# Noisy top-2 experts on one core: a round's last sums and product written behind the next round's first copy

## The chip, the cores and the metric

The kernel runs on one core of one Trainium2 chip. Times are device microseconds (us) of one execution; the figure for a kernel is the median of its runs. The engines are TensorE (PE, with its weight loads as PEld), VectorE (DVE), ScalarE (ACT), GpSimd (POOL) and SyncE (SP, which issues DMAs here).

## What is computed

Three layers follow each other on 2304 tokens of width 512: windowed attention, a gated MLP, and a mixture of eight experts of which each token takes two. The change lies in the third layer alone:

```
def _moe2_ref(x, w_gate, w_noise, noise, w1, w2):
    noisy_logits = x @ w_gate + np.log1p(np.exp(x @ w_noise)) * noise
    top2 = np.argpartition(-noisy_logits, 2, axis=1)[:, :2]
    ...                                   # top2_w: softmax over the two
    for e in range(E):                    # 8 experts, w1[e]: 512 x 1024, w2[e]: 1024 x 512
        for k in range(2):
            mask = top2[:, k] == e
            h = np.maximum(x[mask] @ w1[e], 0.0)
            out[mask] += top2_w[mask, k, None] * (h @ w2[e])
```

Matrix operands are held as a pair, a rounded high part and the remainder ("hi" and "lo"), and each product is three matmuls: hi·hi, hi·lo, lo·hi.

## The kernel before, in words

Each expert takes up to 608 rows (five blocks j = 0 to 4 of 128, the last of 96). They are gathered from DRAM by GpSimd (`gather`), turned by TensorE into columns (`gt`: four 128x128 transposes a block, copied out by ScalarE at L916), multiplied by w1 and put through a relu into `h2` (tile hTa), multiplied by w2 (`p2`, 24 matmuls a block with 512 columns, L315 to L317), scaled into the rows read back from the output (L970, or L972 for expert 0) and scattered (L974).

Expert 0 computes its first product directly (`p1(0, f, groups)`, L932). Blocks 0 to 2 are done by then; what stands here is group 1 (blocks 3 and 4): eight tiles f, each 12 matmuls of 224 columns, a ScalarE relu (L938) and a VectorE remainder (L939).

Experts 1 to 7 use a scheme with seven products in place of eight (`Seven`). Rows and weights are halved both ways; `sums` (L1169 to L1172) makes four sums of row quarters, `operands` (L1116 on ScalarE, then L1117 on VectorE) splits them into hi and lo, and `prep` does the same for the weights: a w1 tile has four small sums on VectorE (L1144 to L1147) and four splits, a w2 tile has two splits. `some(n)` writes the next n pieces of prepared weight work into the order. A product P1 to P7 is six matmuls of 304 columns (L1191). `Seven.p1(e, i)` is one **round** of seven products; an expert has four rounds. Their results combine by accumulation in PSUM and by copies on ScalarE:

- P1 into bank A; ScalarE copies A to B_ (L1208), since P6 then goes on adding into A and P2 adds into B_.
- P7 into Z; ScalarE copies it to an SBUF buffer `u` (L1213).
- After P6, A is copied to C (L1216); P4 adds into C. After P5, A is copied to D_ (L1222); P3 adds into D_.
- Four outputs: B_ itself; A plus the copy of Z (L1223 on VectorE); C plus the copy of Z (L1226); D_. Each gets a relu on ScalarE (L1200) and a remainder on VectorE (L1201).

In the kernel before, a round ends with P4, the sum L1226 and its relu; P3 is written at the end of the round (rounds 0 and 3) or behind the next round's P1 (rounds 1 and 2), with `self.rest` holding its relu. `second(e)` is the stretch between two experts: five blocks of `p2`, the transposes of the next expert's rows, its sums and splits, and three weight tiles of the next expert.

From L1239 on, the orders of TensorE, ScalarE and VectorE are exactly the written order (`manual_schedule`); those of GpSimd and SyncE are set by the scheduler. PSUM has eight banks, given out by `bank(i)`; a new tile in a bank waits for the last reader of the one before it.

Of the kernel before, what the change touches and what calls it, by code (L numbers as in the profile page):

```python
# [9 lines left out]
F32 = mybir.dt.float32  # L10
# [5 lines left out]
AF = mybir.ActivationFunctionType  # L16
OP = mybir.AluOpType
# [12 lines left out]
def tile_alibi_window_attention__swiglu__noisy_top2_moe(  # L30
# [1038 lines left out]
    class Seven:  # L1069
# [3 lines left out]
        def __init__(self):  # L1073
            self.xr = wpool[3].tile([128, KC, CW], F32, name="xr")
            n = 2 * HS
            s = wpool[3].tile([128, 4 * n], F32, name="xs")
            self.s = [s[:, i * n:(i + 1) * n].rearrange("p (c t) -> p c t", c=2) for i in range(4)]
            self.g = [s[:, i * RW:(i + 1) * RW] for i in range(4)]
            u = wpool[3].tile([128, 2 * HS], F32, name="us")
            self.u = [u[:, 0:HS], u[:, HS:]]  # L1080
            self.t = hB[:, PB * DM:PB * DM + 1024].rearrange("p (o k f) -> p o k f", o=4, k=2)
            z = NF2 * CW
            self.wb = [([hT[:, i, z:z + 512] for i in range(2)], [hT[:, i, z + 512:z + 768] for i in range(2)])]
            self.wa, self.w2, self.w2t = [], {}, None
            self.jobs = ([("w1", 1, i) for i in range(3)] +
                         [j for e in range(1, E) for j in
                          [("w2", e, 0), ("w2", e, 1), ("w1", e, 3), ("w2", e, 2), ("w2", e, 3)] + [("w1", e + 1, i) for i in range(3) if e + 1 < E]])
            self.nl = self.nj = 0
            self.rest = lambda: None
            self.todo = []  # L1090
            self.raw = {}
# [39 lines left out]
        def prep(self):  # L1131

            if self.nj == len(self.jobs):
                return
            self.load(self.nj + 1)
            what, e, i = self.jobs[self.nj]
            r = self.raw.pop(self.nj)
            self.nj += 1
            if what == "w1":
                a, b, c = w = self.w1_operands((e - 1) * 4 + i)  # L1140
                t = self.t

                def first():
                    nc.vector.tensor_sub(t[:, 0], r[:, 0:2, 1], r[:, 0:2, 0])  # L1144
                    nc.vector.tensor_sub(t[:, 1], r[:, 2:4, 1], t[:, 0])  # L1145
                    nc.vector.tensor_sub(t[:, 2], r[:, 2:4, 1], r[:, 0:2, 1])
                    nc.vector.tensor_sub(t[:, 3], r[:, 2:4, 0], t[:, 1])  # L1147
                    self.split([a[:, s, 0:2].rearrange("p o k f -> p (o k) f") for s in range(2)], r[:, :, 0])
                self.todo += [first, lambda: self.split([a[:, s, 2:4] for s in range(2)], t[:, 0:2]),
                              lambda: self.split(b, t[:, 2:4]), lambda: self.split(c, r[:, 2:4, 1])]  # L1150
                self.w2["w1", e, i] = w
            else:
                t = place1(0) if i < 3 else self.w2t
                self.todo += [lambda u=u: self.split([t[:, u, s, :] for s in range(2)], r[:, u]) for u in range(2)]
                for u in range(2):
                    self.w2[e, 2 * i + u] = t[:, u]
            f = self.todo.pop()
            self.todo.append(lambda: (f(), self.load(self.nj + 2)))
# [35 lines left out]
        def p1(self, e, i):  # L1194
            A, Z, B_, C, D_ = (bank(x)[:, 0:HS] for x in ((6, 7, 0, 1, 4), (2, 3, 5, 6, 7), (0, 1, 2, 3, 4), (5, 6, 7, 0, 1))[i])
            lo, hi = slice(0, HS), slice(HS, CW)

            def out(ps, f, sl):
                d = h2[0][:, f, sl]
                nc.scalar.activation(d, ps, AF.Relu)  # L1200
                nc.vector.scalar_tensor_tensor(h2[1][:, f, sl], ps, 0.0, f32(d), op0=OP.max, op1=OP.subtract)  # L1201

            def last():
                self.product(e, i, "P3", D_, False)
                self.rest = lambda: out(D_, 4 + i, lo)

            self.product(e, i, "P1", A, True)
            nc.scalar.activation(B_, A, AF.Copy)  # L1208
            if i in (2, 3):
                self.last()  # L1210
            self.rest()
            self.product(e, i, "P7", Z, True)
            nc.scalar.activation(self.u[1], Z, AF.Copy)  # L1213
            self.some(1)
            self.product(e, i, "P6", A, False)
            nc.scalar.activation(C, A, AF.Copy)  # L1216
            self.some(1)
            self.product(e, i, "P2", B_, False)
            out(B_, i, lo)
            self.some(1)  # L1220
            self.product(e, i, "P5", A, False)
            nc.scalar.activation(D_, A, AF.Copy)  # L1222
            nc.vector.tensor_tensor(self.u[0], A, self.u[1], op=OP.add)  # L1223
            out(self.u[0], 4 + i, hi)
            self.product(e, i, "P4", C, False)
            nc.vector.tensor_tensor(self.u[1], C, self.u[1], op=OP.add)  # L1226
            out(self.u[1], i, hi)
            if i in (0, 3):
                last()
                if i == 3:  # L1230
                    self.rest()
                    self.rest = lambda: None
            else:
                self.last = last

    sv = Seven()
    for j in range(CAP):
# [2 lines left out]
    by_hand.__enter__()  # L1240
    for f in range(NF2):
        p1(0, f, (1,))
        if f == 3:
            sv.prep()
        sv.some(1)
    sv.some(9)
    sv.open()

    def second(e):
        n = e + 1  # L1250
        more = n < E
        if more:
            gt(n, 0, bank(6))
            gt(n, 1, bank(7))
        j0 = 0 if e else EARLY
        p2(e, j0, 0, 4)
        if more:
            gt(n, 2, bank(6))
            gt(n, 3, bank(7))
        p2(e, j0, 4, 8)  # L1260
        if more:
            sv.operands(0)
            gt(n, 4, bank(6))
            sv.sums()
            for i in (3, 2):
                sv.operands(i)
        p2(e, j0 + 1)
        if more:
            for i in (1, 5, 4):
                sv.operands(i)  # L1270
            sv.prep()
            sv.some(9)
        for j in range(j0 + 2, CAP):
            p2(e, j)
            if more and j < 4:
                sv.prep()
                sv.some(9)
        if more and e == 0:
            sv.prep()
            sv.some(9)  # L1280

    for j in range(EARLY, CAP):
        prev(0, j)
    second(0)
    for e in range(1, E):
        for i in range(4):
            for _ in range(2 if i == 0 else 1):
                sv.prep()
            sv.p1(e, i)
            if i == 1:  # L1290
                for j in range(CAP):
                    prev(e, j)
                if e + 1 < E:
                    for j in range(CAP):
                        gather(e + 1, j)
        sv.some(9)
        second(e)
    by_hand.__exit__(None, None, None)
    w3p_cm.__exit__(None, None, None)
# [73 lines left out]
```

## Time and profile before

| | |
|---|---|
| median of 3 runs | 1108.96 us (1108.17 to 1109.45) |
| the profiled execution | 1107.09 us, of which the span of instructions is 1105.1 us |
| mean granted TensorE clock | 0.986 |
| PE busy | 1055.2 us, 95% |
| DVE busy | 690.6 us, 62% |
| ACT busy | 560.3 us, 51% |
| POOL busy | 345.1 us, 31% |

The busy shares are of the span. Idle times in the rows further down are those of one engine just before an instruction, with what ended them behind an arrow. A matmul's end in the trace is modelled and reaches into the next matmul's start, so that the distance between two starts, not the sum of busy times, tells the pace. The expert layer fills the span from about 620 us on; the part that the change touches begins with group 1 of expert 0 at 670.65 us.

### The profile page before, as it was taken

To read this page: it belongs to the slowest core of one execution; us is meant where nothing else is said; L and a number is where in the kernel's file an instruction comes from. 1 tells how busy PE (TensorE), PEld (TensorE's weight loads), DVE (VectorE), ACT (ScalarE), POOL (GpSimd) and SP (SyncE) were. 2 spreads that over 40 slices of the span, in tenths; PEclk is the share of its full clock that TensorE was granted. 3 is DMA by queue.
4 is the path that set the end of the run, shared out by engine and by line. 5 is a ranking of instruction groups with operands and counts; after the bars stand their busy time and mean duration, and the time that the engine had idled before them with its cause. 6 is when DMAs were issued, how large, how long until landed. Compare 5 with 4: busy or idle time off the path is not lost. (4 is left out here: it accounts for less than half of the span.)

```text
span 1105.1 us, 18329 instructions
## 1 busy us (share of the span) xinstructions
PE 1055.2 (95%) x6830; PEld 900.2 (81%) x6830; DVE 690.6 (62%) x1546; ACT 560.3 (51%) x1283; POOL 345.1 (31%) x324
## 2 busy tenths in 40 slices
PE   6889999999999999999999999699999999999997
PEld 5667778889988777789997888688888888888885
DVE  6778963577620577325885353868686868686861
ACT  6877854455522455444532323555555555556450
POOL 7300002122233333332377123615151515151211
PEclk9899999999999999999999999899999999999999
DMA  9688745232373233241323503525353535353321
GB/s 213 177 242 271 248 156 185 71 90 72 90 240 124 88 96 100 76 129 58 97 93 104 167 12 102 171 87 177 101 179 107 174 107 176 112 166 120 113 75 41
DMA packets 140259, 143.92 MB, mean 130 GB/s; under 512 B 66510, under 2 KB 109518, under 8 KB 140160
## 3 DMA queue, kind: packets, MB, share of 16 engines
q1 hardware_dynamic: 129776, 113.09, 34.4%
q0 software_dynamic: 9184, 29.26, 8.1%
q8 instruction: 56, 0.92, 0.4%
q10 hardware_dynamic: 1200, 0.30, 0.1%
q14 instruction: 43, 0.35, 0.1%
HBM read 113.84 MB, written 28.91 MB: 129 GB/s over the span
## 5 line engine op out<-in xcount | busy, mean ns | idle before, releaser
L296 POOL TENSOR_TENSOR wu<-wst,wu 128x1024 fp32r<-128x1024 f32 x54 | 129.8, 2404 | 265.7 <-ACT wu L295 240.2
L315 PE MATMUL b<-xT,wu 128*128 128x320 f32 (+1 forms) x576 | 200.0, 351 | 4.6 <-ACT xT L525 4.5
L316 PE MATMUL b<-xT,wu 128*128 128x320 f32 (+1 forms) x576 | 197.5, 343 | 0.1
L317 PE MATMUL b<-xT,wu 128*128 128x320 f32 (+1 forms) x576 | 196.6, 342 | 0.0
L315 PE MATMUL b<-wu,hTa 128*128 128x512 f32 (+1 forms) x482 | 192.1, 401 | 0.0
L316 PE MATMUL b<-wu,hTa 128*128 128x512 f32 (+1 forms) x482 | 189.7, 394 | 0.0
L317 PE MATMUL b<-wu,hTa 128*128 128x512 f32 (+1 forms) x482 | 189.5, 394 | 0.0
L1191 PE MATMUL b<-xT,wu 128*128 128x304 f32 x834 | 128.9, 308 | 21.8 <-ACT b L1208 21.8
L1191 PEld LDWEIGHTS b<-xT,wu 128*128 128x128 f32 x834 | 120.3, 191 | 27.9 <-ACT b L1208 27.0
L295 ACT ACTIVATE wu<-wst 128x1024 fp32r<-128x1024 f32 x80 | 84.4, 1057 | 85.2 <-PE b L317 69.2
L315 PEld LDWEIGHTS b<-xT,wu 128*128 128x128 f32 x576 | 107.8, 188 | 16.8 <-ACT xT L525 5.9
L316 PEld LDWEIGHTS b<-xT,wu 128*128 128x128 f32 x576 | 109.1, 189 | 9.7 <-issue 1.6
L317 PEld LDWEIGHTS b<-xT,wu 128*128 128x128 f32 x576 | 109.0, 189 | 9.0 <-issue 1.5
L317 PEld LDWEIGHTS b<-wu,hTa 128*128 128x128 f32 (+1 forms) x482 | 88.8, 184 | 22.2 <-issue 0.3
L315 PEld LDWEIGHTS b<-wu,hTa 128*128 128x128 f32 (+1 forms) x482 | 88.9, 185 | 21.1 <-issue 0.9
L316 PEld LDWEIGHTS b<-wu,hTa 128*128 128x128 f32 (+1 forms) x482 | 89.1, 185 | 20.8 <-issue 0.6
L610 DVE TENSOR_TENSOR hTa<-sg,hTa 128x320 fp32r<-128x320 f32 (+1 forms) x54 | 69.0, 1283 | 23.0 <-ACT hTa L609 22.9
L974 POOL DMA_INDIRECT out_dram<-hTb,sib x39 | 44.4, 1139 | 98.6 <-DVE hTb L970 64.0
L1117 DVE TENSOR_TENSOR wu<-wst,wu 128x512 fp32r<-128x512 f32 x93 | 61.6, 662 | 21.7 <-ACT wu L1116 21.4
L424 ACT ACTIVATE sx<-sx,mn 128x192 f32<-128x192 f32 (+2 forms) x126 | 53.6, 427 | 41.3 <-DVE mn L421 40.9
L970 DVE SCALAR_TENSOR_TENSOR hTb<-b,wcol,hTb 128x512 f32<-128x512 f32 (+1 forms) x35 | 26.1, 747 | 57.6 <-PE b L317 57.6
L1116 ACT ACTIVATE wu<-wst 128x512 fp32r<-128x512 f32 x93 | 55.4, 600 | 0.0
(244 smaller groups left out, 1834.6 us busy)
## 6 DMA issues: line engine op xcount, KB each, us to landing
wst<-wscr SPq DMA_DIRECT2D x54, 512.0 KB, 3.4
wst<-in_moe_w_dram SPq DMA_DIRECT2D x36, 512.0 KB, 3.8
wst<-in_moe_w_dram SPq DMA_DIRECT2D x56, 256.0 KB, 3.2
wscr<-wst SPq DMA_DIRECT2D x18, 512.0 KB, 3.2
cs<-in_moe_w_gate_dram SPq DMA_DIRECT2D x12, 512.0 KB, 5.0
cs<-in_moe_w_val_dram SPq DMA_DIRECT2D x12, 512.0 KB, 6.3
cs<-in_moe_w_out_dram SPq DMA_DIRECT2D x12, 512.0 KB, 5.3
x2d<-xT SPq DMA_DIRECT2D x18, 256.0 KB, 3.2
```

What stands on the lines that cost most here:

```text
L295: nc.scalar.activation(o[0], s, AF.Copy)
L296: self.eng(n).tensor_sub(o[1], s, f32(o[0]))
L315: nc.tensor.matmul(ps, st(0), mv(0), start=first, stop=False, skip_group_check=True)
L316: nc.tensor.matmul(ps, st(0), mv(1), start=False, stop=False, skip_group_check=True)
L317: nc.tensor.matmul(ps, st(1), mv(0), start=False, stop=last, skip_group_check=True)
L424: a = nc.scalar.activation(x, x, AF.Exp, scale=-1.0, bias=mn[:, i:i + 1], accum_out=sm[:, i:i + 1])
L610: nc.vector.tensor_sub(hh(1, f, sl), t, f32(hh(0, f, sl)))
L970: nc.vector.scalar_tensor_tensor(x, y, wc, x, op0=OP.mult, op1=OP.add)
L974: s = nc.gpsimd.indirect_dma_start(out=out, out_offset=bass.IndirectOffsetOnAxis(ap=R["s"][0:r, col:col + 1], axis=0), in_=x, in_offset=No ...
L1116: nc.scalar.activation(o[0], src, AF.Copy)
L1117: nc.vector.tensor_sub(o[1], src, f32(o[0]))
L1191: nc.tensor.matmul(ps, w[k][:, c], x[:, m, c], start=first and c == 0 and k + m == 0, stop=c == 1 and k == 1, skip_group_check=True)
```

## The change

A round no longer ends with the sum into the second `u`, its relu and (in rounds 0 and 3) P3. These go into `rest`, which the next round runs behind its P1 and the copy L1208; after round 3, `second(e)` runs it behind the first two transposed blocks of the next expert. The copy of Z gets two buffers in turn, so that it lives into the next round. Weight work is spread differently: four preparations in place of five lie in an expert's rounds, and that of w2 tile 3 moves to the start of `second`; the third `some` of a round stands between the sum of A and its relu and is left out in round 1; the first piece of a w1 tile is now the four sums alone with the split of the raw quarter as a piece of its own. At the start, expert 1's rows are transposed between the tiles of expert 0's group 1, and its `sums` and splits follow at once; expert 0's last two blocks of `p2` then run beside the splits of expert 1's rows and weights.

```
@@ Seven.__init__
-            u = wpool[3].tile([128, 2 * HS], F32, name="us")
-            self.u = [u[:, 0:HS], u[:, HS:]]
+            u = wpool[3].tile([128, 3 * HS], F32, name="us")
+            self.u = [u[:, i * HS:(i + 1) * HS] for i in range(3)]
@@ prep
-                    self.split([a[:, s, 0:2].rearrange("p o k f -> p (o k) f") for s in range(2)], r[:, :, 0])
-                self.todo += [first, lambda: self.split([a[:, s, 2:4] for s in range(2)], t[:, 0:2]),
+                self.todo += [first, lambda: self.split([a[:, s, 0:2].rearrange("p o k f -> p (o k) f") for s in range(2)], r[:, :, 0]),
+                              lambda: self.split([a[:, s, 2:4] for s in range(2)], t[:, 0:2]),
                               lambda: self.split(b, t[:, 2:4]), lambda: self.split(c, r[:, 2:4, 1])]
@@ Seven.p1
+            u, z = self.u[0], self.u[1 + i % 2]
-            def last():
+            def rest():
+                nc.vector.tensor_tensor(z, C, z, op=OP.add)
+                out(z, i, hi)
                 self.product(e, i, "P3", D_, False)
-                self.rest = lambda: out(D_, 4 + i, lo)
+                out(D_, 4 + i, lo)
+                self.rest = lambda: None
             self.product(e, i, "P1", A, True)
             nc.scalar.activation(B_, A, AF.Copy)
-            if i in (2, 3):
-                self.last()
             self.rest()
             self.product(e, i, "P7", Z, True)
-            nc.scalar.activation(self.u[1], Z, AF.Copy)
+            nc.scalar.activation(z, Z, AF.Copy)
...
             out(B_, i, lo)
-            self.some(1)
             self.product(e, i, "P5", A, False)
             nc.scalar.activation(D_, A, AF.Copy)
-            nc.vector.tensor_tensor(self.u[0], A, self.u[1], op=OP.add)
-            out(self.u[0], 4 + i, hi)
+            nc.vector.tensor_tensor(u, A, z, op=OP.add)
+            self.some(i != 1)
+            out(u, 4 + i, hi)
             self.product(e, i, "P4", C, False)
-            nc.vector.tensor_tensor(self.u[1], C, self.u[1], op=OP.add)
-            out(self.u[1], i, hi)
-            if i in (0, 3):
-                last()
...
+            self.rest = rest
@@ expert 0's group 1
     for f in range(NF2):
         p1(0, f, (1,))
+        if f in (3, 5):
+            gt(1, f - 3, bank(6))
+            gt(1, f - 2, bank(7))
         if f == 3:
             sv.prep()
-        sv.some(1)
+        if f > 3:
+            sv.some(1)
+        if f == 6:
+            gt(1, 4, bank(6))
+            sv.sums()
     sv.some(9)
     sv.open()
+    sv.operands(0)
+    sv.operands(3)
+    sv.operands(2)
+    prev(0, 3)
+    p2(0, 3)
+    for i in (1, 5, 4):
+        sv.operands(i)
+    sv.prep()
+    sv.some(9)
+    prev(0, 4)
+    p2(0, 4, 0, 4)
+    sv.prep()
+    sv.some(9)
+    p2(0, 4, 4, 8)
@@ second(e), now for e of 1 and above only
+        sv.rest()
+        sv.prep()
+        sv.some(9)
+        p2(e, 0, 0, 4)
...
-            for _ in range(2 if i == 0 else 1):
+            for _ in range((2, 1, 0, 1)[i]):
                 sv.prep()
             sv.p1(e, i)
```

One line is added above `p1`, so that its later lines stand a few numbers further down in the changed kernel: L1208 becomes L1212, L1213 L1215, L1216 L1218, L1222 L1223, L1223 L1224, L1226 L1205, L1200 L1201 and L1201 L1202.

**TensorE from expert 0's group 1 on**, before (a name such as b_6897 is a PSUM bank's tile; the rows of L932 are the tiles f of group 1, those of L913 the transposed blocks of expert 1; xT holds split rows, wu split weights, hTa the remainders and `h2`):

```order
L932 MATMUL b_6897<-xT_6205,wu_6141 128x224 x12
L932 MATMUL b_6914<-xT_6205,wu_6141 128x224 x12
L932 MATMUL b_6931<-xT_6205,wu_6303 128x224 x12
L932 MATMUL b_6954<-xT_6205,wu_6303 128x224 x12
L913 MATMUL b_6971<-ident,xs 128x128 x4
L913 MATMUL b_6978<-ident,xs 128x128 x4
L315 MATMUL b_6985<-wu_6390,hTa 128x512
```

and now:

```order
L913 MATMUL b_6887<-ident,xs 128x128 x4
L913 MATMUL b_6894<-ident,xs 128x128 x4
L932 MATMUL b_6905<-xT_6205,wu_6141 128x224 x12
L932 MATMUL b_6924<-xT_6205,wu_6141 128x224 x12
L913 MATMUL b_6939<-ident,xs 128x128 x4
L913 MATMUL b_6946<-ident,xs 128x128 x4
L932 MATMUL b_6955<-xT_6205,wu_6303 128x224 x12
L913 MATMUL b_6972<-ident,xo_6823 128x96 x4
L932 MATMUL b_6983<-xT_6205,wu_6303 128x224 x12
L315 MATMUL b_7016<-wu_6390,hTa 128x512
```

The five transposed blocks stood in three places, the first of them behind group 1, the others inside `p2`; they now stand between the tiles 3 to 7 of group 1.

**VectorE at the start of expert 1**, before (xr holds the transposed rows, xs their sums, hTb the weight sums, wst raw weights; L972 scales expert 0's block 3):

```order
L972 TENSOR_SCALAR hTb<-b_6985,wcol 128x512
L1117 TENSOR_TENSOR xT_6969<-xr,xT_6969 128x1216
L1169 TENSOR_TENSOR xs<-xr 128x608
L1170 TENSOR_TENSOR xs<-xs,xr 128x608
L1171 TENSOR_TENSOR xs<-xr 128x608
L1172 TENSOR_TENSOR xs<-xr,xs 128x608
```

and now:

```order
L939 SCALAR_TENSOR_TENSOR hTa<-b_6955,hTa 128x224
L1117 TENSOR_TENSOR wu_6904<-hTb,wu_6904 128x512
L1169 TENSOR_TENSOR xs<-xr 128x608
L1170 TENSOR_TENSOR xs<-xs,xr 128x608
L1171 TENSOR_TENSOR xs<-xr 128x608
L1172 TENSOR_TENSOR xs<-xr,xs 128x608
L939 SCALAR_TENSOR_TENSOR hTa<-b_6983,hTa 128x224
L1117 TENSOR_TENSOR hTa<-hTb,hTa 128x512
L1117 TENSOR_TENSOR hTa<-wst,hTa 128x256
L1117 TENSOR_TENSOR xT_7008<-xr,xT_7008 128x1216
```

The four row sums stood behind L972, which reads the finished `p2` of block 3; they now stand between the remainders of expert 0's tiles 6 and 7, and L972 comes after three row splits.

**ScalarE in expert 2, from round 1 into round 2**, before (b_7722 is A of round 1, b_7726 its D_; b_7801, b_7802, b_7803 and b_7804 are A, Z, B_ and C of round 2; us holds the SBUF sums and the copy of Z):

```order
L1222 ACTIVATE b_7726<-b_7722 128x304
L1200 ACTIVATE hTa<-us 128x304 x2
L1208 ACTIVATE b_7803<-b_7801 128x304
L1200 ACTIVATE hTa<-b_7726 128x304
L1213 ACTIVATE us<-b_7802 128x304
L1116 ACTIVATE xT_6970<-hTb 128x512
L1216 ACTIVATE b_7804<-b_7801 128x304
```

and now (b_7713 is A of round 1, b_7717 its D_; b_7793 to b_7796 are A, Z, B_ and C of round 2):

```order
L1223 ACTIVATE b_7717<-b_7713 128x304
L1201 ACTIVATE hTa<-us 128x304
L1212 ACTIVATE b_7795<-b_7793 128x304
L1201 ACTIVATE hTa<-us 128x304
L1201 ACTIVATE hTa<-b_7717 128x304
L1215 ACTIVATE us<-b_7794 128x304
L1116 ACTIVATE wu_7051<-wst 128x512
L1218 ACTIVATE b_7796<-b_7793 128x304
```

The copy of A has moved in front of the second relu from `us`; that relu now stands between the copy of A and the copy of Z. On TensorE the order of this boundary is as before: P4, P1, the old round's P3, P7, P6; from round 0 into round 1 P3 has gone behind P1 as well, and P3 of round 3 behind two transposed blocks.

## Rows read from the trace of the kernel before

**Rows 1.** Waits on TensorE, 690 to 1105 us: total us, times, longest.
```profile
PE b L1191 <- ACT b L1208: 21.8, 21, 8.4
```
**Rows 2.** TensorE's timeline, expert 2's rounds, then expert 7: start, length, instruction, [idle before].
```profile
762.33 0.99 PE L1191 MATMUL b<-xT,wu 128*128 128x304 f32 x6
...
764.00 2.66 PE L1191 MATMUL b<-xT,wu 128*128 128x304 f32 x18
...
775.46 0.99 PE L1191 MATMUL b<-xT,hTa 128*128 128x304 f32 x6
777.92 2.76 PE L1191 MATMUL b<-xT,wu 128*128 128x304 f32 x18 [1.46 <-ACT b L1208]
...
788.46 1.03 PE L913 MATMUL b<-ident,xs 128*128 128x128 f32 x8
789.25 0.48 PE L315 MATMUL b<-wu,hTa 128*128 128x512 f32 x1
...
1058.33 1.94 PE L1191 MATMUL b<-xT,wu 128*128 128x304 f32 x12 [1.47 <-ACT b L1208]
```
**Rows 3.** Timelines of DVE, then ACT, expert 2, from round 1 into round 2.
```profile
775.21 0.47 DVE L1223 TENSOR_TENSOR us<-b,us 128x304 f32<-128x304 f32 x1
...
776.60 0.47 DVE L1226 TENSOR_TENSOR us<-b,us 128x304 f32<-128x304 f32 x1
...
777.10 0.46 ACT L1200 ACTIVATE hTa<-us 128x304 fp32r<-128x304 f32 x1 [0.93 <-DVE us L1226]
777.46 0.41 ACT L1208 ACTIVATE b<-b 128x304 f32<-128x304 f32 x1
```
**Rows 4.** TensorE's timeline, from expert 0's group 1 to the end of expert 1's rounds.
```profile
679.69 2.94 PE L932 MATMUL b<-xT,wu 128*128 128x224 f32 x24 [0.57 <-DVE hTa L939]
...
695.67 0.99 PE L1191 MATMUL b<-xT,wu 128*128 128x304 f32 x6
696.50 1.00 PE L1191 MATMUL b<-xT,hTa 128*128 128x304 f32 x6
705.86 4.93 PE L1191 MATMUL b<-xT,wu 128*128 128x304 f32 x18 [8.35 <-ACT b L1208]
...
732.42 1.03 PE L913 MATMUL b<-ident,xs 128*128 128x128 f32 x8
```
**Rows 5.** Timelines of DVE, then ACT, at the start of expert 1.
```profile
681.72 0.39 DVE L939 SCALAR_TENSOR_TENSOR hTa<-b,hTa 128x224 fp32r<-128x224 f32 x1 [0.58 <-ACT hTa L938]
...
690.72 1.42 DVE L1117 TENSOR_TENSOR xT<-xr,xT 128x1216 fp32r<-128x1216 f32 x1
...
699.38 0.41 DVE L1144 TENSOR_TENSOR hTb<-wst 128x256 f32<-128x256 f32 x1
...
702.04 0.69 DVE L1117 TENSOR_TENSOR xT<-hTb,xT 128x512 fp32r<-128x512 f32 x1
...
702.98 0.42 DVE L1144 TENSOR_TENSOR hTb<-wst 128x256 f32<-128x256 f32 x1
...
704.11 0.42 DVE L1147 TENSOR_TENSOR hTb<-wst,hTb 128x256 f32<-128x256 f32 x1
...
705.40 0.40 ACT L1208 ACTIVATE b<-b 128x304 f32<-128x304 f32 x1
```
**Rows 6.** Stretches: us, busy (instructions) by engine, PEclk, DMA share, GB/s; one PE row.
```profile
69.80:73.20 3.40, 3.40 (x11) 2.33 (x9) 3.40 (x12) 2.71 (x9) 0.82 (x2) 0.51 1.24 212
...
701.20:711.40 10.20, 5.54 (x22) 5.54 (x23) 8.15 (x17) 6.24 (x14) 8.21 (x9) 0.50 0.78 254
...
762.00:789.00 27.00, 25.06 (x176) 24.20 (x175) 18.57 (x38) 17.34 (x42) 7.04 (x6) 1.00 0.53 156
...
69.34 1.35 PE L315 MATMUL b<-xT,wu 128*128 128x512 f32 x3 [2.67 <-ACT xT L525]
```
**Rows 7.** GpSimd's timeline: a gather beside a mostly idle DVE, and one beside splits.
```profile
672.80 0.95 POOL L906 DMA_INDIRECT xs<-x2d,gib  x1 [0.30 <-issue]
...
696.97 3.37 POOL L906 DMA_INDIRECT xs<-x2d,gib  x1 [1.64 <-DVE xT L1117]
```

More of the change, by code (lines that the diff above doesn't have):

```diff
@@ L1219, in p1 @@
             out(B_, i, lo)
-            self.some(1)
             self.product(e, i, "P5", A, False)
             nc.scalar.activation(D_, A, AF.Copy)
-            nc.vector.tensor_tensor(self.u[0], A, self.u[1], op=OP.add)
-            out(self.u[0], 4 + i, hi)
+            nc.vector.tensor_tensor(u, A, z, op=OP.add)
+            self.some(i != 1)
+            out(u, 4 + i, hi)
             self.product(e, i, "P4", C, False)
-            nc.vector.tensor_tensor(self.u[1], C, self.u[1], op=OP.add)
-            out(self.u[1], i, hi)
-            if i in (0, 3):
-                last()
[L1230 to L1234, printed above, removed]
+            self.rest = rest
     sv = Seven()
@@ L1254, in second @@
             gt(n, 1, bank(7))
-        j0 = 0 if e else EARLY
-        p2(e, j0, 0, 4)
+        sv.rest()
+        sv.prep()
+        sv.some(9)
+        p2(e, 0, 0, 4)
         if more:
@@ L1259, in second @@
             gt(n, 3, bank(7))
-        p2(e, j0, 4, 8)
-        if more:
             sv.operands(0)
+            p2(e, 0, 4, 6)
             gt(n, 4, bank(6))
             sv.sums()
+            p2(e, 0, 6, 8)
             for i in (3, 2):
                 sv.operands(i)
-        p2(e, j0 + 1)
+        else:
+            p2(e, 0, 4, 8)
+        p2(e, 1)
         if more:
@@ L1270, in second @@
                 sv.operands(i)
[L1271 to L1275, printed above, removed]
+        for j in range(2, CAP):
+            if more:
                 sv.prep()
                 sv.some(9)
[L1278 to L1284, printed above, removed]
+            p2(e, j)
     for e in range(1, E):
         for i in range(4):
-            for _ in range(2 if i == 0 else 1):
+            for _ in range((2, 1, 0, 1)[i]):
                 sv.prep()
@@ L1295, in tile_alibi_window_attention__swiglu__noisy_top2_moe @@
                         gather(e + 1, j)
-        sv.some(9)
         second(e)
```

## The prediction

> **What bounds the kernel now.** I read three views in this order: TensorE's list of waits, its timeline through the experts, and the timelines of the two engines that it waits for. In the experts TensorE waits for one thing only, ScalarE's copy L1208: 21 waits, 21.8 us [rows 1]. One of them, in expert 1's first round, is 8.35 us [rows 4]; experts 2 to 7 have three each, alike from expert 2 (1.46 the longest) to expert 7 (1.47) [rows 2]. Otherwise TensorE runs without a gap there, so what this layer can give is these waits, what they cost in clock, and 0.57 us in expert 0 [rows 4].
>
> Why the copy is late is seen between rounds 1 and 2 of expert 2 [rows 3]. Its input, P1, was ready before P7 began at 775.46 [rows 2]. But the copy is written behind two relus from `us`; the second waits for VectorE's L1226 (776.60), which stands behind L1223 (775.21) and its remainder. From L1223 to the copy's end is a chain of 777.87 - 775.21 = 2.66 us that the copy does not need.
>
> **Experts 2 to 7.** Pace: 12 matmuls from 762.33 to 764.00 [rows 2], 0.139 us each, 0.835 for a product. Four rounds are 168 matmuls, 23.35 us; from the first product to the transposes they take 788.46 - 762.33 = 26.13 [rows 2]. The excess, 2.78, is the three waits: the profile counts 1.94 idle, but modelled matmul ends hide part (P7, begun at 775.46, is issued by 776.29, and the next starts at 777.92: 1.63, not 1.46). The change writes the copy directly behind P1, with P3 (0.835) and P7 (0.835) on TensorE before P6 needs it; a copy of 0.41 [rows 3] fits with 1 us to spare. The first round has only P7 in between, as before, where it caused no wait. So 6 x 2.78 = 16.7 us go, if nothing else is late.
>
> What is late next: relu of the second sum, relu of D_, copy of Z, a split and the copy L1216 now follow each other on ScalarE, in that order, and P5 waits for the last. From L1223's start to that relu's start 1.89 us, then 0.36 by [rows 3] for each of relu, relu and copy, at most 0.69 for a split (the VectorE split of [rows 5]) and 0.41: 4.1 at most. P5 to the next P5 is six products, 5.0. With VectorE free L1223 starts about 0.5 after P5 (behind the copy to D_), which leaves 0.4. In round 1 the weight sums, 1.55 us from 702.98 to the end of 704.11 [rows 5], are in front of it; before the change L1223 was 2.2 us behind P5 there (775.21 against 775.46 - 3 x 0.835 = 773.0, P4, P1 and P3 lying between P5 and P7), with two splits more in the queue. Less 2 x 0.6 that is 1.0 behind, and the margin is about nought. I take nothing for it, because ScalarE's split should be shorter than my bound; the other end is 0.5 us in each of seven experts, 3.5.
>
> Moved beside this, each at nothing: P3 of round 3 and its relu go behind the first transposes of `second`; the 12 matmuls of `p2` that follow need neither, and cover the relus. W2 tile 3, two splits, moves to the same place and is needed six matmuls later still; its load is issued by SyncE in the same order as before, a round earlier than its use. If that cover were gone, `p2` would wait for at most the two splits, 1.4 us an expert by [rows 5]. The third `u` buffer costs only space. GpSimd's gathers for the next expert wait for the same row splits, and still have four rounds to land.
>
> **Expert 0 and the start of expert 1.** Transposes between the tiles of group 1 give L939 time: the 0.57 goes, and I count 0.6. TensorE then reaches expert 1's first product at 695.67 - 0.6 = 695.1 and has issued P1 and P7 by 696.7, since its amount of work is unchanged.
>
> L1208 of round 0 does not get there so early. ScalarE writes it behind the splits of two w1 tiles, and these follow VectorE's chain, which I add up from the same instructions in the old order. The remainder of tile 6 started at 681.72 [rows 5]; without the 0.6 and with two pairs of transposes in front (0.79 each, 788.46 to 789.25 [rows 2]) it starts at 682.7. With it (0.39) and one split (0.6) the row sums can start at 683.6. From 690.72 to 699.38 VectorE did the row splits, the row sums and one L972 without a pause: 8.66 us; the same instructions stand in the new order. The remainder of tile 7 adds 0.3, the last two splits of w1 tile 0 0.94 (702.04 to 702.98), w1 tile 1 3.60 (699.38 to 702.98), and the sums of tile 2 1.55 [all rows 5]. That is 683.6 + 8.66 + 0.3 + 0.94 + 3.60 + 1.55 = 698.65. ScalarE's last splits and L1208 follow as they did: from the end of L1147 at 704.53 to the end of L1208 at 705.80, 1.27 [rows 5]. So P6 starts at about 699.95, and TensorE stands from 696.7: 3.25 us, where by the same count it stood from 697.33 to 705.86, 8.5. VectorE, not TensorE, is the bound of this stretch.
>
> **The clock.** Behind the 8.35 us TensorE ran at 1.2 GHz: from 701.2 to 711.4 the granted clock is 0.50, with 5.54 us of matmuls in it [rows 6], of which half, 2.8 us, is lost. Will 3.25 us still do that? Early in the trace 2.67 us of idling was followed by 3.4 us at 0.51 [rows 6]; the 1.46 in expert 2 was followed by nothing, its clock is 1.00 [rows 6]. The new gap is longer than one that cost the clock, so I take one such stretch, half of 3.4: 1.7 us. Bounds are 0 and the 2.8 of before.
>
> The Trainium skill (TensorE: Matmul & The Clock Gate, section "A second HAM failure mode: psum-queue depth-cycling") says that short idle times between groups of matmuls cycling through PSUM banks make the clock swing. By that rule the three short waits of every expert would cost clock too, and removing them would give more than 16.7. The trace disagrees: clock 1.00 through expert 2 [rows 6], so nothing is added.
>
> Expert 1's rounds took 732.42 - 695.67 = 36.75 [rows 4], 13.4 over 23.35. Of that 3.25 + 1.7, and 0.1 for a restart, stay: 8.35 go.
>
> **The sum.** 16.7 + 8.35 + 0.6 = 25.6 us. The profiled execution took 1107.09 (span 1105.1 and 2 around it) and would take 1081.5. It lies 1.9 below the median of the runs, 1108.96; from the median the sum gives 1083.4.
>
> **The rivals.**
> 1. The opening's gap leaves the clock alone: 1.7 less, 1081.7. For it: 1.46 did; against it: 2.67 did not.
> 2. The margin in round 1 fails: ScalarE's chain makes P5 wait up to 0.5 us an expert. 1083.4 + 2 (half of that to 3.5) = 1085 to 1087.
> 3. VectorE pays for GpSimd. A gather beside splits took 3.37, one beside a mostly idle VectorE 0.95 [rows 7]. If the difference, 2.4, came out of VectorE for each of the four row gathers in the new chain, the gap would grow by up to 9.7, to 1093. Against it: within that long gather (697 to 700.3) VectorE's 256-column sum at 699.38 took 0.41, the same as 0.42 at 702.98 and 704.11 [rows 5]; GpSimd pays. The Trainium skill (GPSIMD Engine Reference, section 1, Specifications) says that the two share their SBUF interfaces, with contention when VectorE reads two SBUF inputs; it does not say who pays.
> 4. The wait only changes its instruction: P5 for L1216 in place of P6 for L1208, of the same size. Then only expert 0 and 1 gain: 1108.96 - 9 = 1100. Against it: the chain counted above ends before P5 is due, or at it.
> 5. Slower: ScalarE works strictly in order, so the relu of the second sum, now ahead of the copies of Z and A, would stop both in every later round. It decides from 1.2 us that P5 waits in each of the 21 later rounds (25.6 / 21); at 1.6 us the time is 1109 - 25.6 + 21 x 1.6 = 1117. For it: in-order queues made the old wait. Against it: VectorE has less in front of that sum than before.
>
> **How the numbers follow.** Forecast as summed, 0.60; rival 1 0.15; rival 2 0.13; rival 3 0.05; rival 4 0.03; no visible change 0.01; rival 5 0.03. About 0.2% (2.2 us) is what a measurement of this kernel can tell from no change. So faster 0.96, same 0.01, slower 0.03. The range: 1080.5 (rival 1, with the opening a little shorter) to 1089 (rival 2 in full, with the clock's 2.8); rivals 3 to 5 are left out.
>
> **What would show it.** In the changed profile: no wait for L1212 (the old L1208) but one, about 3.2 us, in expert 1 near 700; then about 3.4 us at half clock; 22.5 us from an expert's first product to the next transposes in experts 2 to 7 (162 matmuls, P3 having gone behind them) in place of 26.1; no wait of TensorE on L1218. A wait on L1218 once an expert is rival 2; longer VectorE operations beside gathers are rival 3. The prediction is wrong if TensorE waits for anything else in the rounds, or if `p2` begins to wait for splits that were moved in front of it.

## The result, and the profile after

The changed kernel takes 1081.83 us (1081.56 to 1082.98, four runs) against 1108.76 (1108.17 to 1109.45) for the kernel before, run beside it: the ratio is 0.9759, 95% interval 0.9742 to 0.9776, or 26.9 us less. The forecast was 1083.4 with a range of 1080.5 to 1089. A second measurement beside other runs of the kernel before gave 1084.4 against 1110.11, 25.7 us less; the sum in the prediction was 25.6. Its terms did not come out singly as well as this, as the last sections show.

TensorE's list of waits after, 664 us to the end (total us, times, longest), answers [rows 1]:

```profile
PE b L1191 <- ACT b L1212: 3.4, 1, 3.4
```

The 21 waits are one. L1212 is the old L1208, and the one that stays is in expert 1's first round. TensorE's timeline of expert 2, then expert 7's first product, after (start, length, instruction):

```profile
754.46 0.99 PE L1191 MATMUL b<-xT,wu 128*128 128x304 f32 x6
...
756.13 2.66 PE L1191 MATMUL b<-xT,wu 128*128 128x304 f32 x18
758.63 1.00 PE L1191 MATMUL b<-xT 128*128 128x304 f32 x6
...
766.99 0.99 PE L1191 MATMUL b<-xT,hTa 128*128 128x304 f32 x6
767.82 2.74 PE L1191 MATMUL b<-xT,wu 128*128 128x304 f32 x18
770.40 1.00 PE L1191 MATMUL b<-xT,hTa 128*128 128x304 f32 x6
...
777.08 1.03 PE L913 MATMUL b<-ident,xs 128*128 128x128 f32 x8
777.87 0.52 PE L1191 MATMUL b<-xT 128*128 128x304 f32 x2
...
778.79 0.40 PE L315 MATMUL b<-wu,hTa 128*128 128x512 f32 x1
...
1021.34 0.99 PE L1191 MATMUL b<-xT,wu 128*128 128x304 f32 x6
```

From the first product to the transposes it is 777.08 - 754.46 = 22.62 us, where [rows 2] gave 26.13. No row has an idle time. Five experts lie between 754.46 and 1021.34: 53.38 us each. Before, four of the same five took 56.04 each and one took 56.24. P3 of round 3 now stands behind the transposes (777.87 to 778.79).

The boundary between rounds 1 and 2 of expert 2, on DVE and then ACT, answers [rows 3] (L1224 and L1205 are the sums L1223 and L1226 of before; L1201 the relu; L1218 the copy of A that P5 waits for):

```profile
765.61 0.46 DVE L1224 TENSOR_TENSOR us<-b,us 128x304 f32<-128x304 f32 x1
...
766.99 0.47 DVE L1205 TENSOR_TENSOR us<-b,us 128x304 f32<-128x304 f32 x1
```
```profile
766.11 0.46 ACT L1201 ACTIVATE hTa<-us 128x304 fp32r<-128x304 f32 x1 [0.96 <-DVE us L1224]
766.47 0.41 ACT L1212 ACTIVATE b<-b 128x304 f32<-128x304 f32 x1
767.49 0.46 ACT L1201 ACTIVATE hTa<-us 128x304 fp32r<-128x304 f32 x1 [0.61 <-DVE us L1205]
...
768.46 0.63 ACT L1116 ACTIVATE wu<-wst 128x512 fp32r<-128x512 f32 x1
768.98 0.42 ACT L1218 ACTIVATE b<-b 128x304 f32<-128x304 f32 x1
```

ScalarE still waits for VectorE's second sum, but L1212 has left 1 us before that. It still stands behind the relu of the first sum (766.11), so a late L1224 would delay it as before; where VectorE does its weight work therefore still counts. Now the opening, TensorE's timeline, answering [rows 4]:

```profile
673.18 5.80 PE L932 MATMUL b<-xT,wu 128*128 128x224 f32 x48
678.82 1.03 PE L913 MATMUL b<-ident,xs 128*128 128x128 f32 x8
...
697.40 0.99 PE L1191 MATMUL b<-xT,wu 128*128 128x304 f32 x6
698.23 1.00 PE L1191 MATMUL b<-xT,hTa 128*128 128x304 f32 x6
702.63 2.77 PE L1191 MATMUL b<-xT,wu 128*128 128x304 f32 x18 [3.39 <-ACT b L1212]
705.23 1.00 PE L1191 MATMUL b<-xT,hTa 128*128 128x304 f32 x6
...
723.69 1.03 PE L913 MATMUL b<-ident,xs 128*128 128x128 f32 x8
```

The gap is 3.39 us where it was 8.35, and behind it 18 matmuls run from 702.63 to 705.23, 2.60 us, at full speed. The stretches say the same (us, then busy time and instructions of PE, PEld, DVE, ACT and POOL, PEclk, DMA share, GB/s); they answer [rows 6]:

```profile
702.60:706.00 3.40, 3.37 (x24) 3.38 (x25) 3.29 (x7) 2.65 (x7) 0.88 (x2) 1.00 0.90 318
...
754.00:781.00 27.00, 27.00 (x189) 26.42 (x188) 19.45 (x41) 19.49 (x46) 6.52 (x6) 1.00 0.49 148
```

Laid side by side, with the starts of [rows 2, 4] and of the rows above, in us (the end is the span's, 1105.1 and 1080.9):

| stretch | before | after | forecast | measured |
|---|---|---|---|---|
| start to group 1 of expert 0 | 670.65 | 673.18 | 0 | +2.53 |
| group 1 to expert 1's first product | 25.02 | 24.22 | -0.6 | -0.80 |
| that to expert 2's first product | 66.66 | 57.06 | -8.35 | -9.60 |
| that to the end | 342.77 | 326.44 | -16.7 | -16.33 |

The first line is not the change's: its code is untouched, and over the fourteen traces of this study, before's and after's among them, it runs from 669.9 to 673.2.

### The profile page after: what moved, and what is told of

It reads as the page before. It is cut to its first block, busy times and chain, and to the rows that moved or that the text cites. A ratio compares the mean times of both kernels' runs of the same rounds, so it can differ in the third digit from the quotient of the medians.

```text
span 1080.9 us, 18357 instructions
## 1 busy us (share of the span) xinstructions
PE 1050.7 (97%) x6830; PEld 900.0 (83%) x6830; DVE 691.5 (64%) x1546; ACT 563.2 (52%) x1283; POOL 336.0 (31%) x324
## 4 chain that ended last, share of the span: by engine, by line
PE 93%; DVE 3%; ACT 3%; issue 1%; DMA 0%; POOL 0%; ACTq 0%; POOLq 0%; DVEq 0%
PE b L315 21%; PE b L316 21%; PE b L317 21%; PE b L1191 15%; PE b L510 3%; PE b L932 2%; PE b L480 2%; PE b L463 2%; PE b L913 2%; PE b L378 1%; PE b L446 1%; PE b L698 1%; PE b L711 1%; ACT sx L424 1%; DVE xT L1117 1%
## 5 line engine op out<-in xcount | busy, mean ns | idle before, releaser
L1191 PE MATMUL b<-xT,wu 128*128 128x304 f32 x834 | 124.8, 303 | 3.4 <-ACT b L1212 3.4
L610 DVE TENSOR_TENSOR hTa<-sg,hTa 128x320 fp32r<-128x320 f32 (+1 forms) x54 | 68.9, 1282 | 22.9 <-ACT hTa L609 22.9
L1117 DVE TENSOR_TENSOR wu<-wst,wu 128x512 fp32r<-128x512 f32 x93 | 61.1, 664 | 24.2 <-ACT wu L1116 23.3
L608 DVE SCALAR_TENSOR_TENSOR sg<-sg,b 128x320 f32<-128x320 f32 (+1 forms) x72 | 39.5, 549 | 23.4 <-PE b L317 22.9
```

Of the source, the lines that this page charges most:

```text
L608: nc.vector.scalar_tensor_tensor(t, t, 0.5, ps[:, :w_], op0=OP.mult, op1=OP.mult)
L610: nc.vector.tensor_sub(hh(1, f, sl), t, f32(hh(0, f, sl)))
L1117: nc.vector.tensor_sub(o[1], src, f32(o[0]))
L1191: nc.tensor.matmul(ps, w[k][:, c], x[:, m, c], start=first and c == 0 and k + m == 0, stop=c == 1 and k == 1, skip_group_check=True)
```

## The experiments

Three theories are told apart. **A**, the forecast's: the wait was made by the copy's place behind a relu that follows VectorE; the spread of the weight work and the second buffer only have to keep the next chain on ScalarE short enough. **B**: only one of the change's parts brings the gain, and the rest is ornament. **C**, on the opening: TensorE's time there goes with the length of the gap alone, against the forecast's that a half-clock stretch follows it. Each set below was run on one chip beside runs of the kernel before; differences are taken from medians within a set. Besides, the *round figure* is the distance from expert 2's first product to the transposes, 26.13 before and 22.62 after.

### The two halves apart

rounds_only: the new rounds and the new `second` for experts 1 to 7, but expert 0's group 1 and the stretch into expert 1 written as before, except that `prep` stays changed, so that the weight work comes there in the new pieces.

```
@@ expert 0's group 1
-        if f in (3, 5):
-            gt(1, f - 3, bank(6))
-            gt(1, f - 2, bank(7))
...
+    opening(0)          # the old second(0)
```

> Expert 0's group 1 and the start of expert 1 in the old order, the rounds and the stretches between experts in the new one. If the two halves of the change act in separate places, expert 1's first wait for the copy of A is back at about 8.4 us with TensorE at half clock behind it (8.5 - 3.6 of standing, 2.8 of clock, 0.8 in group 1: 8.5 us in all), and no round of experts 2 to 7 waits: 1081.8 + 8.5 = 1090.3. If instead the new opening also fed the later rounds (rows, weights or gathers arriving sooner), waits of the old size come back in experts 2 to 7 and the time goes towards 1106.

opening_only: the new stretch from group 1 to expert 1, with the old rounds, the old split of the weight work and the old `second`.

> The new opening with the rounds, the weight work and the stretches between experts of the kernel before. Separate places: the opening waits about 2.8 to 3.4 us, every expert has its three waits for L1208 again (0.3, 1.5 and 0.2 by the profile, 2.7 with what hides behind the modelled ends; 2.2 in expert 1): 1081.8 + 6 x 2.7 + 2.2 = 1100. If the rounds were helped by the opening, it is below 1095.

Measured: rounds_only 1087.01 us, 20.8 below before; opening_only 1098.5, 9.3 below. The waits of TensorE from 690 us on, rounds_only first, opening_only second:

```profile
PE b L1191 <- ACT b L1212: 8.4, 1, 8.4
```
```profile
PE b L1191 <- ACT b L1208: 16.3, 22, 2.8
```

Each half removes its own waits and leaves the other's. The round figure of rounds_only is 22.62, of opening_only 26.13. Alone they save 30.1, together 26.9. From group 1 to the end the traces give 20.0 and 8.6 against 26.7 together, 1.9 apart. Of that 0.63 is the opening gap, 2.76 us with the old spread of weight work and 3.39 with the new; 0.57 is the wait of [rows 4] on L939, which is gone in both halves and so counted twice. The clock takes part as well: behind the same gap rounds_only has 2.96 us of matmuls at half clock (701.2 to 708.0) where the kernel before has 5.54 [rows 6], so that 1.3 us less is lost, and nothing shows that an edit did that. Against these stands a third short wait of expert 1 in opening_only, which the kernel before has not (22 waits against 21). The rest was not taken apart.

The wait on L939 in group 1 goes by a different way in each half. VectorE there, in the kernel before, in rounds_only and in opening_only (L1117 is the first split of expert 1's w1 tile 0):

```profile
678.65 0.68 DVE L1117 TENSOR_TENSOR wu<-wst,wu 128x512 fp32r<-128x512 f32 x1
679.25 0.38 DVE L939 SCALAR_TENSOR_TENSOR hTa<-b,hTa 128x224 fp32r<-128x224 f32 x1
```
```profile
678.44 0.38 DVE L939 SCALAR_TENSOR_TENSOR hTa<-b,hTa 128x224 fp32r<-128x224 f32 x1
678.74 0.68 DVE L1117 TENSOR_TENSOR wu<-wst,wu 128x512 fp32r<-128x512 f32 x1
```
```profile
680.23 0.68 DVE L1117 TENSOR_TENSOR wu<-wst,wu 128x512 fp32r<-128x512 f32 x1
680.84 0.38 DVE L939 SCALAR_TENSOR_TENSOR hTa<-b,hTa 128x224 fp32r<-128x224 f32 x1
```

Before, a tile's remainder L939 stands behind the four weight sums and their first split, which are one piece, and TensorE waits for it at 679.69. In rounds_only the split is a piece of its own and comes behind the remainder, and all 96 matmuls of group 1 run without a wait:

```profile
670.44 11.37 PE L932 MATMUL b<-xT,wu 128*128 128x224 f32 x96
```

In opening_only the remainder stands behind the split as before, but transposes stand between the tiles on TensorE, and no wait for L939 is left either.

### The three parts of the new rounds

copy_late: the change, but with the second sum's relu back in front of the copy of A.

```
-            def rest():
+            def early():
                 nc.vector.tensor_tensor(z, C, z, op=OP.add)
                 out(z, i, hi)
...
             self.product(e, i, "P1", A, True)
+            self.early()
             nc.scalar.activation(B_, A, AF.Copy)
```

> The changed kernel with one thing undone: the sum into the second us buffer and its relu stand in front of the copy of A to B_ again, P3 and the weight work stay as changed. If the place of the copy on ScalarE is what the old waits were, P6 waits for it in rounds 1 to 3, but less than before since round 1 has less weight work: about 0.15, 0.5 and 0.15 us by the distance of starts and 0.1 for each restart, 1.0 to 1.1 an expert, 1081.8 + 7 = 1089. If the spread of the weight work was the cause and the copy's place is free, it stays within 1 us of 1081.8.

old_spread: the change, with the weight work where it was (five preparations in the rounds, the third `some` ahead of the copy to D_, the first piece of a w1 tile with its split).

```
             out(B_, i, lo)
+            self.some(1)
             self.product(e, i, "P5", A, False)
...
-            self.some(i != 1)
...
-            for _ in range((2, 1, 0, 1)[i]):
+            for _ in range(2 if i == 0 else 1):
```

This undoes three things at once, and they were not tried one by one.

> The changed kernel with the old spread of the weight work: three pieces in every round with the third in front of P5, five preparations in an expert's rounds, none moved to the stretch between experts, the four sums and the first split one piece. If the copy's place alone did it, no round waits and the time is 1081.8. If the new order has a margin of about a tenth of a us, as I counted for round 1, one more split on ScalarE and the sums with it on VectorE break it: waits for the copy of A (about 0.4) and for the copy to C (about 0.9) at the start of round 2 in each expert, 1.5 with the restarts, 1081.8 + 10 = 1092.

one_buffer: the change, with one buffer for the copy of Z.

```
-            u, z = self.u[0], self.u[1 + i % 2]
+            u, z = self.u[0], self.u[1]
```

> The changed kernel with a single buffer for the copy of Z. The copy then has to wait until the old round's sum in that buffer has been read by VectorE's remainder, one step of about 0.5 us behind the relu, with the relu of D_ beside it. If the margin of round 1 into round 2 is as thin as counted (about 0.1), P5 waits about 0.4 us for the copy to C once an expert, 0.5 with the restart: 1081.8 + 7 x 0.5 = 1085.2. If the margin is 0.5 us or more, no change: 1081.8.

It was run again beside the changed kernel itself:

> One buffer for the copy of Z again, beside the changed kernel on the same chip. Its first profile showed TensorE waiting for the copy L1218 once an expert, 0.26 us each. If these waits are all that the edit costs, it is 0.3 to 0.5 us an expert above the changed kernel, 2 to 3.5 us; if the 6.1 us measured across two sessions belong to the edit, it is 6 above.

| kernel | median, us | below before, same set | round figure |
|---|---|---|---|
| copy_late | 1087.77 | 20.0 | 23.52 |
| old_spread | 1089.79 | 18.0 | 23.94 |
| one_buffer | 1089.27 | 20.8 | 23.22 |
| one_buffer_2 | 1088.71 | 21.4 | 23.22 |
| changed kernel, beside one_buffer_2 | 1084.4 | 25.7 | 22.62 |

All three parts are needed: undoing one costs 0.90, 1.32 and 0.60 us an expert, though the first alone is what the change's main step is about. One_buffer's edit costs 4.3 us beside the changed kernel, which is 7 x 0.60; the 6 us of its first run, against another set, were too many.

How each does it. TensorE and ScalarE of copy_late, expert 2, where round 2 begins (L1217 is the copy of A there):

```profile
766.72 1.00 PE L1191 MATMUL b<-xT,hTa 128*128 128x304 f32 x6
767.91 2.77 PE L1191 MATMUL b<-xT,wu 128*128 128x304 f32 x18 [0.20 <-ACT b L1217]
770.52 1.00 PE L1191 MATMUL b<-xT,hTa 128*128 128x304 f32 x6
```
```profile
767.09 0.46 ACT L1201 ACTIVATE hTa<-us 128x304 fp32r<-128x304 f32 x1 [0.93 <-DVE us L1205]
767.46 0.41 ACT L1217 ACTIVATE b<-b 128x304 f32<-128x304 f32 x1
```

The same 0.93 as in [rows 3]: the copy stands behind a relu that waits for VectorE. P7 to P6 takes 767.91 - 766.72 = 1.19 in place of 0.835, so 0.36 is lost, of which the profile counts 0.20. The other two boundaries (759 to 767 and 773 to 777) lose 0.25 each against the changed kernel's starts, and the profile counts nothing there. Its eight waits sum to 4.8 us, 3.4 of them in the opening; what the experts lose is 7 x 0.90 = 6.3.

old_spread's waits from 690 us on, and TensorE in expert 2 (L1213 is the copy of A, L1219 the copy that P5 needs):

```profile
PE b L1192 <- ACT b L1213: 4.2, 8, 2.8
PE b L1192 <- ACT b L1219: 4.2, 7, 0.6
```
```profile
768.93 1.93 PE L1192 MATMUL b<-xT,wu 128*128 128x304 f32 x12 [0.20 <-ACT b L1213]
771.46 1.10 PE L1192 MATMUL b<-xT,wu 128*128 128x304 f32 x6 [0.59 <-ACT b L1219]
```

Here the rival that the prediction called "the margin fails" is seen in full: P5 waits for L1219, once an expert, in the round behind the weight sums. In one_buffer_2 it is the same place with another cause (TensorE, then ScalarE):

```profile
770.36 1.83 PE L1191 MATMUL b<-xT,wu 128*128 128x304 f32 x12
772.46 1.10 PE L1191 MATMUL b<-xT,wu 128*128 128x304 f32 x6 [0.27 <-ACT b L1218]
```
```profile
771.15 0.42 ACT L1215 ACTIVATE us<-b 128x304 f32<-128x304 f32 x1 [0.29 <-DVE hTa L1202]
```

The copy of Z waits 0.29 for VectorE to have read the old copy, and this goes on through the split and L1218 to P5. So theory A holds, with a stronger condition than the forecast gave it, and B falls.

### The opening: gap and clock

early_weights: expert 1's weight splits begin two tiles of group 1 sooner, two pieces at a time, so that less stands in front of L1212. (The places for a w1 tile's last two splits are looked up only when these are written, for `open` makes some of them later than the tile's first pieces now come.)

```
-        if f == 3:
+        if f == 1:
+            sv.prep()
+        if f in (2, 3, 4):
+            sv.some(2 if f < 4 else 1)
+        if f == 4:
             sv.prep()
-        if f > 3:
-            sv.some(1)
+        if f in (5, 6):
+            sv.some(f - 4)
...
-    sv.some(9)
     sv.open()
...
     for i in (1, 5, 4):
         sv.operands(i)
-    sv.prep()
     sv.some(9)
```

> The changed kernel with the weight work of expert 1 begun sooner: w1 tile 0 behind expert 0's tile 1 (two tiles sooner), and the sums and first splits of w1 tile 1 beside tiles 5 and 6, where VectorE has idle time. If the opening's wait of 3.4 us is VectorE's chain, as summed, about 3 us of it go (two splits of tile 0, the sums of tile 1 and two of its splits leave the chain): a wait of 0.3 to 0.6 us, 1081.8 - 3 = 1078.8. If the wait is set by something else, such as the landing of data or the finished rows of expert 0, it stays at 1081.8.

gap_5 and gap_7: four and eight sums more on VectorE in the opening's chain, ahead of the sums of w1 tile 2 and overwritten by them.

```
                 def first():
+                    for _ in range(1 if (e, i) == (1, 2) else 0):    # gap_7: 2
+                        for o in range(4):
+                            nc.vector.tensor_sub(t[:, o], r[:, 0:2, 1], r[:, 0:2, 0])
```

> The changed kernel with VectorE's opening chain made longer on purpose: four more weight sums of 256 columns (computed and then overwritten) in front of those of expert 1's w1 tile 2, 1.4 us. The wait of TensorE in the opening grows from 3.4 to 4.8 us one for one if VectorE's chain sets it. For the clock: if such a gap is still too short to cost it, the time is 1081.8 + 1.4 = 1083.2 and the granted clock stays at 1.00; if it costs it as the 8.35 us did, 1.7 to 2.8 more, 1085 to 1086.

> As the run before with eight more sums, 2.8 us: the wait is about 6.2 us. Clock untouched: 1084.6. Clock lost behind it: 1086.3 to 1087.4, and half the granted clock in a stretch near 700 us of the profile. If the wait grows by less than the added sums, something else than VectorE's chain is also late there.

Then the changed kernel, early_weights and gap_5 once more, beside one_buffer_2:

> The changed kernel once more, unaltered. If the late relus of expert 0's group 1 (L938 0.8 and 1.6 us behind their matmuls, TensorE waiting 1.1 us for L939), seen in all four kernels that were run together with one_buffer, come with the chip or the run, they may show here too or be absent from all of this group; if they come with those edits, they are absent here and present in the three others, although one_buffer's program is the same as this one up to expert 1's first round. Time: 27 us below the kernel before, as measured. Clock after the opening gap of 3.4 us: open; 1.00 as in the first profile, or half for 3.4 us as in one_buffer.

> Expert 1's weights split sooner, again, beside the changed kernel on the same chip. If the opening's stand of TensorE (3.4 us in the changed kernel, 0.4 here) is worth its length, this is 3.0 below the changed kernel; if half-clock stretches follow the 3.4 us gap in part of the executions, up to 1.7 more.

> Four sums more in the opening's chain, again, beside the changed kernel on the same chip. The gap grows by 1.35 us (4.74 against 3.39 in the first profile). If the gap alone counts, it is 1.4 above the changed kernel; if it brings the half clock of 6.8 us that its first profile showed, and the changed kernel has none, 3.4 more, 4.7 above.

The gap before P6 in expert 1 in each profile, and the time at half clock that begins in it (sampled in slices of 0.6 us):

| kernel | gap, us | at half clock, us |
|---|---|---|
| early_weights, early_weights_2 | 0.37, 0.39 | 0, 0 |
| opening_only, old_spread | 2.76, 2.79 | 0, 0 |
| after, copy_late | 3.39, 3.38 | 0, 0 |
| one_buffer, one_buffer_2, after_again | 3.39 each | about 3.4 each |
| gap_5, gap_5_2 | 4.74 each | about 6.8 each |
| gap_7, rounds_only | 6.07, 8.36 | about 6.8 each |
| before | 8.35 | about 10.2 |

Three of five gaps of 3.4 us cost the clock and two did not. The changed kernel has done both: the row of the first profile stands above; this is the second, after_again (timeline of TensorE, then the stretch):

```profile
700.58 4.17 PE L1191 MATMUL b<-xT,wu 128*128 128x304 f32 x18 [3.39 <-ACT b L1212]
704.58 0.99 PE L1191 MATMUL b<-xT,hTa 128*128 128x304 f32 x6
```
```profile
700.20:703.60 3.40, 3.02 (x12) 3.02 (x13) 2.56 (x6) 2.12 (x6) 0.55 (x3) 0.51 0.84 300
```

The 18 matmuls take 704.58 - 700.58 = 4.00 us against 2.60: the clock costs 1.40 there. So neither C nor the forecast is right for every execution; which way a gap of this length goes was not found.

Times: early_weights 1080.3 (29.8 below before) and early_weights_2 1080.39 (29.7 below); the second is 4.0 below the changed kernel beside it (1079.57 to 1081.07 against 1083.82 to 1085.82), and so beats both kernels of this case. Its trace shows the wait that is left (the line is that of P6's product):

```profile
699.00 2.78 PE L1196 MATMUL b<-xT,wu 128*128 128x304 f32 x18 [0.39 <-ACT b L1217]
```

3.0 us of gap and 1.40 of clock are gone, and with them a pause of after_again that is shown below. gap_5 took 1086.81 (23.3 below before), gap_7 1087.21 (22.9), gap_5_2 1084.86 (25.3), which is 0.5 above the changed kernel beside it; 1.4 or 4.7 was expected. Its five runs lie apart (three at 1084.7 to 1084.9, two at 1087.5 and 1088.1), so that the 0.5 is uncertain by more than its size. From expert 1's first product to expert 2's it takes 60.71 against 59.93 in after_again, 0.78 more: 1.35 of gap and about 1 of clock (4.85 us of matmuls in its half-clock stretch against 3.02, half of each lost), less a pause in after_again that gap_5_2 has not. This is that pause, on L1218, with a second one, on L939 (after_again's waits of TensorE from 664 us on, then ScalarE in group 1 and in expert 1):

```profile
PE b L1191 <- ACT b L1212: 3.4, 1, 3.4
PE b L1191 <- ACT b L1218: 1.3, 1, 1.3
PE b L932 <- DVE hTa L939: 1.0, 1, 1.0
```
```profile
675.13 0.36 ACT L938 ACTIVATE hTa<-b 128x224 fp32r<-128x224 f32 x1 [1.72 <-PE b L932]
678.04 0.36 ACT L938 ACTIVATE hTa<-b 128x224 fp32r<-128x224 f32 x1 [2.56 <-PE b L932]
...
716.42 0.41 ACT L1218 ACTIVATE b<-b 128x304 f32<-128x304 f32 x1 [1.31 <-PE b L1191]
```

In the first profile of the same program these two relus started 1.34 us apart, as the tiles do, L1218 followed the split in front of it without a pause, and neither wait was there. The late relus are in all eight profiles of the last two sets, whatever the edit, and in none of the first set, before's or after's. The profile names no cause: the matmuls that they read were long done. It stays open.

## Why the prediction was right, and where not

**Experts 2 to 7: right.** 16.7 forecast, 16.33 measured. An expert gained 2.66 us (56.04 less 53.38) where 2.78 was forecast. Of the 0.12, 0.08 is a wait of P5: P6 to P4 in round 2 takes 2.58 us (767.82 to 770.40) in place of 2.50 (756.13 to 758.63). P3 behind the transposes takes 0.92 (777.87 to 778.79) in place of 0.835, but this is no loss: the first matmul of `p2`, which stood there before and took 0.31 to the next start (789.25 to 789.56), now takes 0.24 (778.79 to 779.03). The sum came out closer than its parts because one expert of the profile before was 0.2 longer than the others, and because expert 7, with no transposes behind it, gained 2.8.

**The margin of round 1: right, and as thin as said.** The chain was put at 4.1 us, from L1224's start to the end of L1218; it took 769.40 - 765.61 = 3.79, with 1.88 to the relu (1.89 forecast) and a split of 0.52 from start to start where the bound was 0.69. L1224 came 1.1 us behind P5 (P5 started about 5.0 before 769.5), 1.0 was forecast. P5 waits 0.08 as a result. What the prediction did not see is that this "nought" is bought by three parts: it gave the new copy's place the whole gain and called the third buffer mere space ("costs only space"). That is true of its cost, but without it 0.60 an expert goes, and without the spread 1.32.

**Expert 0: right.** 0.80 measured, 0.6 forecast, because transposes would give L939 time. opening_only shows it: the order of VectorE is the old one there and the wait is gone. What the prediction did not see is that the new pieces of `prep` take the wait away by themselves, as rounds_only shows. The 1.0 us on L939 in after_again has another cause, the late relu in front of it.

**The opening's chain: right.** VectorE's sum gave 3.25 us in which TensorE stands; by starts it is 702.63 - 698.23 - 0.835 = 3.56, of which 3.39 are counted. The kernels with the old spread of weight work have 2.76 and 2.79, so the new spread costs 0.6 of it here, which the prediction did not price.

**The clock: the mis-sized term.** 1.7 lost was forecast; the first measurement lost nothing, after_again 1.40. That is why expert 1 gained 9.60 and not 8.35 (8.35 + 1.7, less 0.3 for the longer gap and about 0.1 that an expert fell short elsewhere), and why 1081.83 lies on the first rival's 1081.7. Half of the stretch was too much even where it came, since TensorE still stood in the first 0.4 us of it.

**Luck in the total.** That 25.7 was measured the second time, with 25.6 forecast, is in part luck. From group 1 to the end the kernel before took 434.4 us in its profile, the changed kernel 407.7 in its first and 412.0 in after_again: 26.7 less and 22.4 less. The 4.3 between the two are 1.2 in front of expert 1, 1.4 of clock and 1.5 at the pause behind L1218, and in these two executions an earlier start of group 1 (669.90 against 673.18) makes up most of it. The kernel before has one profile, without the late relus; what it would lose with them is not known.

**The other rivals.** The wait did not move to L1218 (no such row in the first profile, and one in after_again, in expert 1 alone and behind a pause of ScalarE, so rivals 4 and 5 fall); the margin's rival came down to 0.08 an expert. VectorE did not pay for GpSimd: in the changed kernel a scatter beside sums took 2.40 us at 695.03 and one at 755.68 took 0.94, while the sum L1145 inside the first (696.59) took 0.42, like L1144 at 710.37 with GpSimd idle. The Trainium skill (GPSIMD Engine Reference, section 1, Specifications) names an SBUF interface shared by the two, with contention when VectorE reads two SBUF inputs. That table does not say who waits; in these rows it is GpSimd whose instruction is longer.

**The rule that was weighed.** opening_only keeps the three short waits of every expert, and its stretch of expert 2 reads:

```profile
754.00:781.00 27.00, 25.05 (x177) 24.27 (x176) 19.07 (x39) 17.35 (x42) 7.05 (x6) 1.00 0.50 150
```

The clock is 1.00. The Trainium skill (TensorE: Matmul & The Clock Gate, section "A second HAM failure mode: psum-queue depth-cycling") says that short idle times between groups of matmuls, where they are frequent enough, swing the clock. Three waits in 56 us, of up to 1.5 us each, did not, before the change and in this half of it.

## What to carry to other kernels

When an engine works strictly in written order, look for an instruction whose input is ready and which stands behind one that waits for a third engine: moving it forward here gave 2.66 us an expert, but only together with what shortened the queue behind it, so undo each part alone before calling one of them the cause, and look up what else the comparison kernel still has of the change (rounds_only had the new pieces). Measure stalls of TensorE by the distance between starts, since the counted idle time showed 0.2 of 0.9 us. And do not take the name in a list of waits for a cause: L939 was late by 0.57 us because a split stood in front of it, and by 1.0 in after_again because a relu came late, and only the timelines of VectorE and ScalarE tell the two apart.

## What had not been expected of the hardware

Equal gaps of 3.39 us on TensorE, in the same place of the same program, were followed by full clock in one execution and by some 3.4 us at half clock in another; in the expert layer of these fourteen profiles the gaps of 2.8 and less did not cost it, and those of 4.7 and more did, for 6.8 to 10.2 us. After a wait a row of 18 matmuls took 2.60 us to the next start in place of 2.50 (702.63 to 705.23 against 756.13 to 758.63), so that the wait cost TensorE about 0.1 us beyond its length. And ScalarE started relus up to 2.3 us later than in the first profile of the same program (678.04 - 669.90 = 8.14 behind group 1's start against 679.02 - 673.18 = 5.84), for no reason that the profile shows.
